# Windowed attention and two FFNs on one core: another layout of K^T, and other steps for the weight conversion

## The chip, the cores and the metric

The kernel runs on one core of a Trainium2 chip. The metric is the device time of one execution in microseconds. Three timed runs of the kernel before gave 912.32, 913.23 and 914.58 us; the median is 913.23.

## The reference

Three stages stand behind one another. Attention has 4 batches of 8 heads, 512 local and 32 global positions and a head size of 64. Local queries see the 32 global keys and the local keys at a distance of at most 32; global queries see all 544 keys.

```python
s_g = scale * q_g @ k_all^T ;  out_g = softmax(s_g) @ v_all
s_ll = where(|i - j| <= 32, scale * q_l @ k_l^T, -1e9)
s_lg = scale * q_l @ k_g^T
out_l = softmax(concat[s_lg, s_ll]) @ concat[v_g, v_l]
x = concat[out_g, out_l], as 2176 rows of 512
x = (h * cos(h)) @ w_out,  h = x @ w_in           # first FFN, 512 -> 2048 -> 512
y = relu(h)^2 @ w2_out,    h = x @ w2_in          # second FFN
```

The FFN weights come as 64-bit floats, and the kernel makes 32-bit floats of them itself ("conversion").

## The kernel before

**Attention.** A pair p is two heads of one batch; there are 16. Its work is split into items: two local items (each 256 queries of both heads) for every pair, and after two pairs one global item (the global queries of four heads). So 40 items stand in a list, ten for each batch: L L L L G L L L L G. The loop at the end of the kernel runs over steps s. In each step every kind of work is issued once, for the item or pair that lies `lag` places away, in the order of `CFG["order"]`: CV (copies of V, shifted by half a block), LQ (Q loads), S (scores on TensorE, here PE), TE (evacuation of the transposed probabilities by ScalarE, here ACT), BG (conversion: loads and part A), LK (K loads), OM (output matmuls), TRK (transposes of K), KEV (evacuation of K^T), CC (conversion part C), SM (masked scores and exps), RC (reciprocals), NM (norm), CB (conversion part B), LV (V loads), OE (output evacuation), TRQ and QE (transposes of Q and their evacuation), KC (K^T's other parts), TM (transposes of probabilities). Each engine works through its own queue in that order. Nothing overtakes on an engine: what stands behind a waiting instruction waits too.

With the lags, an item's scores are computed in step s, its norm is issued in s+1, its transposes on PE in s+2 and their evacuation on ACT in s+3, its output matmuls in s+4. K loads are issued for every second pair in steps 0, 5, 10 and so on, Q loads (four transfers) in steps 1, 6, 11, V loads (six) in steps 3, 8, 13, the copies of V in steps 1, 6, 11. In steps 5, 15 and 25 the V of the global tokens is loaded for the next batch, in 4, 14, 24 a small load for K's tail and in 7, 17, 27 the global queries (L397). All these loads and copies are issued by SP's queue, in program order.

**K^T.** `kT` holds 8 blocks of 160 columns for a pair: 64 keys of the block, 64 of the next block (a copy), 32 global keys. ACT writes the first 64 of each block out of PSUM (L336). GpSimd, here POOL, copies seven blocks into the second 64 (L351), broadcasts the global keys (L353) and copies the tail (L361). A score matmul reads the 160 columns of a block at once (L420). The local keys are laid out shifted by 32, so that a block and the next make the window of 64 queries.

**Probabilities.** VectorE (DVE) adds the mask and finds the row's extremum into `pt`, ACT takes the exponential in place with its sum (L446). The norm multiplies by the reciprocal: POOL for the global 32 columns into `pg` (L468), then the 128 window columns in place, one unit on DVE and three on POOL (L475). PE transposes them into `tw` (L488), in one of two PSUM banks that K's, Q's and the global items' transposes use too; ACT evacuates it into `tws` (L494) and `tg` into `tgs` (L498). There are four buffers of `pt`.

**Conversion.** The weights are cut into 32 groups g of two pieces each. `Feed.begin` starts at most one piece in a call and moves a pipeline of five stages: the load is issued in the step of the beginning (L126, L131), part A (POOL L143, ACT L146) two steps later, part B (DVE L154, L155) three, part C (POOL L165) four steps later. There are two buffers of the raw piece. In attention a step adds 0.5 to a credit from step 5 on, but not in steps of which the fifth next begins a new pair (`free`); a piece starts at 1.0. That gives pieces 8, 11, 14, 18, 21, 24, 28, 31, 34, 36 and 38, named here by the step of their beginning. From step 40 on FFN steps run in the same loop and add 0.5 each as well. A converted group is split into a high and a low part in two calls of `split`: two ACT copies (L228), then in a later call one subtraction on POOL and one on DVE (L214). In attention `split` is called in steps 22, 24, 27, 29 and 33; it returns where the group isn't converted.

**FFN.** 160 steps of 24 matmuls each (L757, L786), the first four of them within the attention loop. The first group of four weight groups serves five column blocks, 20 steps.

Of the kernel before, what the change touches and what calls it, by code (L numbers as in the profile page):

```python
# [10 lines left out]
F32 = mybir.dt.float32  # L11
# [3 lines left out]
AF = mybir.ActivationFunctionType  # L15
ALU = mybir.AluOpType
# [3 lines left out]
P = 128  # L20
NEG = -8.0e9
# [22 lines left out]
         'CV': 11},  # L44
 'ndv': 1,
 'teg': 'AA',
 'free': -5,
 'kb': 'P',
 'split': [22, 24, 27, 29, 33],
 'sx': [32, 34, 37, 39],  # L50
 'arate': 0.5,
 'rate': 0.5,
 's0': 5,
 'groups': [[4, 5, 7], [8, 8]],
 'xd': [0, 1, 2, 3],
 'nr': 6,
 'oe': 'DD',
 'sgb': 0}
GROUPS = CFG["groups"]
RATE, ARATE, XD, NRING = CFG["rate"], CFG["arate"], CFG["xd"], CFG["nr"]  # L60

@with_exitstack
def kernel(
# [14 lines left out]
    nc = tc.nc  # L78
# [175 lines left out]
    ep = early.enter_context(tc.tile_pool(name="ep", bufs=1))  # L254

    KTB = 2 * 64 + SG
    masks = [ep.tile([P, 160], F32, name=f"mask{i}") for i in range(3)]
    VA = [lp.tile([P, 5, 4, D], F32, name=f"va{i}") for i in range(2)]
    VB = [lp.tile([P, 4, 4, D], F32, name=f"vb{i}") for i in range(2)]
# [61 lines left out]
    def tr_k(p):  # L321
        b, kk = divmod(p, NPAIR)
        tk = bank(BT, "tk")
        for c in range(4):
            nc.tensor.transpose(  # L325
                tk[:, c * P : (c + 1) * P],
                kn[p // 2][:, c, 2 * (p % 2) : 2 * (p % 2) + 2].rearrange("p h d -> p (h d)"),
                ident,
            )
        t = ep.tile([P, 8, KTB], F32, tag="kT", name="kT", bufs=3)  # L330
        kT[p] = t
        tks[p] = tk

    def k_evac(p):
        t, tk = kT[p], tks.pop(p)
        nc.scalar.activation(  # L336
            t[:, :, 0:64], tk.rearrange("p (j q) -> p j q", q=64), AF.Copy
        )
        if CFG["kb"] == "A":
            nc.scalar.activation(  # L340
                t[:, :, 128:KTB], tk[:, 0:SG].unsqueeze(1).to_broadcast([P, 8, SG]), AF.Copy
            )
        elif CFG["kb"] == "D":
            nc.vector.tensor_copy(
                t[:, :, 128:KTB], tk[:, 0:SG].unsqueeze(1).to_broadcast([P, 8, SG])
            )

    def k_copy(p):
        t = kT[p]
        one = dict(scalar1=1.0, scalar2=1.0, op0=ALU.mult, op1=ALU.mult)  # L350
        nc.gpsimd.tensor_scalar(t[:, 0:7, 64:128], t[:, 1:8, 0:64], **one)  # L351
        if CFG["kb"] == "P":
            nc.gpsimd.tensor_scalar(  # L353
                t[:, :, 128:KTB], t[:, 0, 0:SG].unsqueeze(1).to_broadcast([P, 8, SG]), **one
            )
        if p > 1:
            k_tail(p)

    def k_tail(p):
        b, kk = divmod(p, NPAIR)  # L360
        nc.gpsimd.tensor_scalar(  # L361
            kT[p][:, 7, 64:128], ktail[:, kk, b, :], 1.0, 1.0, op0=ALU.mult, op1=ALU.mult
        )

    def tr_q(p):
# [37 lines left out]
        load_small(qgn, q_g[b], b)  # L403

    class Local:
# [4 lines left out]
        def s_mm(self):  # L413
            self.s = [bank(BS, "s") for h in range(2)]
            for i in range(2):
                for half in range(2):
                    j = 4 * self.hb + 2 * i + half
                    for h in range(2):
                        d = slice(64 * h, 64 * h + 64)
                        nc.tensor.matmul(  # L420
                            self.s[h][64 * half : 64 * half + 64, 160 * i : 160 * i + 160],
                            lhsT=qT[self.p][d, 64 * j : 64 * j + 64],
                            rhs=kT[self.p][d, j, :],
                            start=True,
                            stop=True,
                            skip_group_check=True,
                        )

        def softmax(self):
            self.pt = lp.tile([P, 4, KTB], F32, tag="pt", name="pt", bufs=4)  # L430
            self.st = lp.tile([P, 3, 4], F32, tag="st", name="st", bufs=4)

            def unit(u):
                i = 2 * self.hb + u % 2
                m = masks[1] if i == 0 else masks[2] if i == 3 else masks[0]
                nc.vector.tensor_tensor_reduce(  # L436
                    out=self.pt[:, u, :],
                    in0=self.s[u // 2][:, 160 * (u % 2) : 160 * (u % 2) + 160],
                    in1=m,
                    scale=-0.125,  # L440
                    scalar=3.0e38,
                    op0=ALU.add,
                    op1=ALU.min,
                    accum_out=self.st[:, 0, u : u + 1],
                )
                nc.scalar.activation(  # L446
                    self.pt[:, u, :],
                    self.pt[:, u, :],
                    AF.Exp,
                    bias=self.st[:, 0, u : u + 1],  # L450
                    scale=-1.0,
                    accum_out=self.st[:, 1, u : u + 1],
                )

            return [lambda u=u: unit(u) for u in range(4)]
# [10 lines left out]
        def norm(self):  # L466
            self.pg = lp.tile([P, 4, SG], F32, tag="pg", name="pg", bufs=2)
            nc.gpsimd.tensor_tensor(  # L468
                self.pg,
                self.pt[:, :, P:KTB],  # L470
                self.st[:, 2, :].unsqueeze(2).to_broadcast([P, 4, SG]),
                op=ALU.mult,
            )
            for u in range(4):
                (nc.vector if u < CFG["ndv"] else nc.gpsimd).tensor_scalar(  # L475
                    self.pt[:, u, 0:P],
                    self.pt[:, u, 0:P],
                    self.st[:, 2, u : u + 1],
                    1.0,
                    op0=ALU.mult,  # L480
                    op1=ALU.mult,
                )

        def t_mm(self):
            self.tw = bank(BT, "tw").rearrange("p (u q) -> p u q", u=4)
            self.tg = bank(BG, "tg")[:, 0:P]
            for u in range(4):
                nc.tensor.transpose(self.tw[:, u, :], self.pt[:, u, 0:P], ident)  # L488
            nc.tensor.transpose(self.tg, self.pg.rearrange("p u q -> p (u q)"), ident)

        def t_evac(self):
# [42 lines left out]
    class Global:  # L534
# [3 lines left out]
        def s_mm(self):  # L538
            self.s = []
            for n in (320, 256):  # L540
                s = bank(BT if CFG["sgb"] >> (n == 256) & 1 else BS, "sg")
                self.s.append(s)
                for i in range(2):
# [2 lines left out]
                    nc.tensor.matmul(  # L546
                        s[64 * i : 64 * i + 64, 0:n],
                        lhsT=qgbd[:, kk, self.b, :],
                        rhs=t[:, 0:5, 0:64] if n == 320 else t[:, 5:8:2, 0:128],
                        start=True,  # L550
                        stop=True,
                    )
# [96 lines left out]
    for h in range(2):  # L649
# [3 lines left out]
            compare_op=ALU.is_ge, fill=NEG, base=0, channel_multiplier=-1,  # L653
        )
        nc.gpsimd.affine_select(
            out=masks[0][s, 64:128], in_=masks[0][s, 64:128], pattern=[[-1, 64]],
            compare_op=ALU.is_ge, fill=NEG, base=0, channel_multiplier=1,
        )
    for i in (1, 2):
        nc.vector.tensor_copy(masks[i], masks[0])  # L660
    nc.vector.memset(masks[1][0:64, 0:32], NEG)
    nc.vector.memset(masks[2][64:128, 96:128], NEG)
    nc.vector.memset(qgbd, 0.0)

    nc.gpsimd.memset(ktail, 0.0)
# [238 lines left out]
    for s in range(L["TRK"], NI + L["OE"]):  # L904
        due = lambda k: due_tr.get(s - k)
        cb, qe = [], []
        for c in CFG["order"]:
            if c == "BG":
                cb = feed.begin(ARATE if due(CFG["free"]) is None else 0.0) if s >= CFG["s0"] else []
            elif c == "CB":  # L910
                for op in cb:
                    op()
# [111 lines left out]
```

## Time and profile before

| | |
|---|---|
| median of the timed runs | 913.23 us (912.32 to 914.58) |
| the profiled execution's own time | 911.74 us |
| its span | 910.0 us |
| PE busy | 890.7 us (98%) |
| weight loads of PE | 793.7 us (87%) |
| DVE, ACT, POOL busy | 502.5, 439.4, 447.8 us |
| chain that ended last, by engine | PE 91%, DVE 3%, DMA 2% |

The span is what the trace covers. A row of a timeline has the start and the length in microseconds from the span's start, the engine, the line of the kernel, the operation, what it writes and reads, the shape and how many instructions are merged; in brackets stands the idle time of its engine before it and what ended that. SPq is SP's queue, where transfers are issued; the length of such a row is the issue alone, not the transfer. A busy PE isn't PE at its peak, since matmuls are pipelined and their ends are modelled.

### The profile page before, as it was taken

The numbers are of one execution on the slowest core, as the hardware profiler recorded it, in microseconds if no ns is written. First come the engines' busy times: TensorE is split into PE (matmuls) and PEld (weight loads), VectorE is DVE, ScalarE is ACT, GpSimd is POOL, SyncE is SP. The second block draws the span as 40 slices with busy tenths as digits, with TensorE's granted clock in tenths as the row PEclk, the third lists the DMA queues.
The fourth block names the chain that finished last, engine by engine and source line by source line (L and its number), as shares of the span: only waits on it lengthen the run. The fifth ranks groups of instructions, "written<-read, shape, count | busy, mean of one in ns | idle before, by whom it ended". The sixth has DMA issues, their size and how long they took to land.

```text
span 910.0 us, 15436 instructions
## 1 busy us (share of the span) xinstructions
PE 890.7 (98%) x5720; PEld 793.7 (87%) x5720; DVE 502.5 (55%) x1058; ACT 439.4 (48%) x1036; POOL 447.8 (49%) x517
## 2 busy tenths in 40 slices
PE   7899999999999999999999999999999999999997
PEld 5777777999999999999999988889999888899996
DVE  5687899866776666765554483433422833232221
ACT  5778787665655545545444553333334632222211
POOL 4577888754574435744342484444423842222221
PEclk9999999999999999999999999999999999999999
DMA  7888643221122111121110021111100101010001
GB/s 168 192 192 195 165 129 94 71 70 53 49 62 70 47 53 61 50 70 47 47 47 1 1 70 47 53 44 66 47 1 1 47 1 47 1 47 1 35 35 36
DMA packets 82075, 57.10 MB, mean 63 GB/s; under 512 B 58320, under 2 KB 74704, under 8 KB 82000
## 3 DMA queue, kind: packets, MB, share of 16 engines
q1 hardware_dynamic: 79824, 55.59, 22.0%
q8 instruction: 45, 0.74, 0.3%
q10 hardware_dynamic: 2176, 0.52, 0.3%
q14 instruction: 30, 0.25, 0.1%
HBM read 47.45 MB, written 4.46 MB: 57 GB/s over the span
## 4 chain that ended last, share of the span: by engine, by line
PE 91%; DVE 3%; DMA 2%; ACT 1%; SPq 1%; POOL 1%; issue 1%; ACTq 0%; POOLq 0%; DVEq 0%
PE h L757 41%; PE y L786 41%; PE s L420 2%; PE tw L488 1%; PE o L504 1%; PE tq L368 1%; DVE pt L436 1%; PE o L516 1%; PE og L622 1%; DMA raw<-in_moe_w_out_dram 1%; PE sg L546 1%; PE tk L325 0%; ACT pt L446 0%; SPq L292 0%; PE twg L603 0%
## 5 line engine op out<-in xcount | busy, mean ns | idle before, releaser
L757 PE MATMUL h<-x,w 128*128 128x436 f32 (+3 forms) x1920 | 403.4, 358 | 0.0
L857 POOL TENSOR_TENSOR glo<-cr,ghi 128x436 fp32r<-128x436 f32 (+3 forms) x160 | 186.8, 1167 | 407.7 <-ACT ghi L851 393.9
L757 PEld LDWEIGHTS h<-x,w 128*128 128x128 f32 x1920 | 354.6, 188 | 27.5
L786 PE MATMUL y<-ghi,w 128*128 128x436 f32 (+1 forms) x640 | 177.6, 358 | 0.0
L846 DVE TENSOR_TENSOR cr<-h,cr 128x436 f32<-128x436 f32 (+3 forms) x160 | 96.6, 605 | 134.0 <-ACT cr L837 115.0
L786 PE MATMUL y<-w,ghi 128*128 128x512 f32 x544 | 168.4, 390 | 0.0
L745 DVE TENSOR_TENSOR x<-xt,x 128x436 fp32r<-128x436 f32 (+3 forms) x100 | 102.5, 1035 | 93.3 <-ACT x L744 78.3
L837 ACT ACTIVATE cr<-h 128x384 f32<-128x384 f32 (+1 forms) x80 | 42.8, 535 | 210.7 <-PE h L757 209.4
L786 PEld LDWEIGHTS y<-ghi,w 128*128 128x128 f32 x640 | 120.3, 188 | 6.1
L786 PEld LDWEIGHTS y<-w,ghi 128*128 128x128 f32 x544 | 101.4, 188 | 18.9
L786 PE MATMUL y<-glo,w 128*128 128x436 f32 (+1 forms) x320 | 114.8, 359 | 0.0
L786 PE MATMUL y<-w,glo 128*128 128x512 f32 x272 | 106.8, 393 | 0.0
L851 ACT ACTIVATE ghi<-cr 128x436 fp32r<-128x436 f32 (+3 forms) x160 | 89.7, 560 | 24.5 <-DVE cr L846 23.6
L831 ACT ACTIVATE ck<-h 128x436 int32<-128x436 f32 (+1 forms) x80 | 42.6, 532 | 113.1 <-PE h L757 113.1
L833 DVE SCALAR_TENSOR_TENSOR cr<-h,ck 128x436 f32<-128x436 f32 (+1 forms) x80 | 48.6, 607 | 84.9 <-ACT ck L831 84.9
L165 POOL TENSOR_TENSOR r<-cu,cc 128x512 uint32<-128x512 uint32 x64 | 85.0, 1328 | 2.0 <-DVE cc L155 2.0
L744 ACT ACTIVATE x<-xt 128x436 fp32r<-128x436 f32 (+3 forms) x100 | 55.1, 560 | 20.2 <-PE h L757 19.9
L786 PEld LDWEIGHTS y<-glo,w 128*128 128x128 f32 x320 | 60.1, 188 | 2.7
L786 PEld LDWEIGHTS y<-w,glo 128*128 128x128 f32 x272 | 51.0, 188 | 10.8
L842 ACT ACTIVATE cr<-cr,halfpi 128x436 f32<-128x436 f32 (+1 forms) x80 | 52.5, 657 | 10.1 <-DVE cr L833 10.1
L155 DVE SCALAR_TENSOR_TENSOR cc<-raw,cc 128x512 uint32<-128x512 uint32 x64 | 55.7, 870 | 0.0
L446 ACT ACTIVATE pt<-pt,st 128x160 f32<-128x160 f32 x128 | 53.3, 425 | 4.1 <-DVE st L436 4.1
(91 smaller groups left out, 907.4 us busy)
## 6 DMA issues: line engine op xcount, KB each, us to landing
raw<-in_moe_w_in_dram SPq DMA_DIRECT2D x32, 512.0 KB, 3.7
raw<-in_moe_w_out_dram SPq DMA_DIRECT2D x32, 512.0 KB, 3.5
vb<-va SPq DMA_DIRECT2D x16, 256.0 KB, 4.6
out_dram<-ypart SPq DMA_DIRECT2D x16, 256.0 KB, 2.1
qn<-in_q_l_dram SPq DMA_DIRECT2D x28, 128.0 KB, 3.7
va<-in_v_l_dram SPq DMA_DIRECT2D x24, 128.0 KB, 3.3
kn<-in_k_l_dram SPq DMA_DIRECT2D x21, 128.0 KB, 3.0
va<-in_v_l_dram SPq DMA_DIRECT2D x8, 96.0 KB, 3.2
```

Source lines behind the costliest of these rows:

```text
L155: lambda: v.scalar_tensor_tensor(c, t[:, :, 1].bitcast(U32), 0x80000000, c, op0=ALU.bitwise_and, op1=ALU.bitwise_or,),
L165: nc.gpsimd.tensor_tensor(ring[g][:, q, :].bitcast(U32), u, c, op=ALU.add)
L446: nc.scalar.activation(self.pt[:, u, :], self.pt[:, u, :], AF.Exp, bias=self.st[:, 0, u : u + 1], scale=-1.0, accum_out=self.st[:, 1, u : ...
L744: nc.scalar.activation(hi, xr, AF.Copy)
L745: return lambda: (nc.vector if kk in XD else nc.gpsimd).tensor_tensor(lo, xr, hi.bitcast(F32), op=ALU.subtract)
L757: nc.tensor.matmul(h, lhsT=w[:, ws, 0, kk * P : (kk + 1) * P], rhs=x, start=(k == 0), stop=(k == 3 * NK - 1),)
L786: nc.tensor.matmul(o, lhsT=l, rhs=r, start=(c_first and k == 0), stop=(c_last and k == 2))
L833: lambda: nc.vector.scalar_tensor_tensor(r, h, INV2PI, k, op0=ALU.mult, op1=ALU.subtract),
L842: nc.scalar.activation(ctmp[s], ctmp[s], AF.Sin, bias=halfpi, scale=TWOPI)
L846: nc.vector.tensor_tensor(r, hps.pop(s), r, op=ALU.mult)
L851: nc.scalar.activation(ghi[s], ctmp[s], AF.Copy)
L857: nc.gpsimd.tensor_tensor(lo, ctmp.pop(s), hi.bitcast(F32), op=ALU.subtract)
```

## The change

K^T becomes one row of nine places of 96 columns: 64 keys of a block and 32 global keys behind them. A score matmul reads 160 columns from the start of a place: the block, the global keys, and the next block. So blocks are no longer copied; the ninth place holds the tail. The masks and `pt` follow that order (64, 32, 64), `pt` gets a fifth unit of space and three buffers instead of four. The norm of the window columns writes to a new tile `pn` (two buffers), which the transposes read.

The conversion's beginnings in attention are now a list of steps, and the calls of `split` move. From step 40 on the attention loop begins no piece any more, only the FFN steps do.

```diff
- 'free': -5,
- 'split': [22, 24, 27, 29, 33],
+ 'split': [15, 21, 25, 31, 35],
- 'arate': 0.5,
+ 'begin': [6, 9, 14, 16, 19, 24, 26, 29, 34, 36],
- 's0': 5,
...
+    GK = slice(64, 64 + SG)
...
-        t = ep.tile([P, 8, KTB], F32, tag="kT", name="kT", bufs=3)
+        t = ep.tile([P, 9, 64 + SG], F32, tag="kT", name="kT", bufs=3)
...
     def k_evac(p):
         nc.scalar.activation(
-            t[:, :, 0:64], tk.rearrange("p (j q) -> p j q", q=64), AF.Copy
+            t[:, 0:8, 0:64], tk.rearrange("p (j q) -> p j q", q=64), AF.Copy
         )
...
     def k_copy(p):
-        nc.gpsimd.tensor_scalar(t[:, 0:7, 64:128], t[:, 1:8, 0:64], **one)
-        if CFG["kb"] == "P":
-            nc.gpsimd.tensor_scalar(
-                t[:, :, 128:KTB], t[:, 0, 0:SG].unsqueeze(1).to_broadcast([P, 8, SG]), **one
-            )
+        nc.gpsimd.tensor_scalar(
+            t[:, 0:8, GK], t[:, 0, 0:SG].unsqueeze(1).to_broadcast([P, 8, SG]), **one
+        )
...
     def k_tail(p):
-            kT[p][:, 7, 64:128], ktail[:, kk, b, :], 1.0, 1.0, op0=ALU.mult, op1=ALU.mult
+            kT[p][:, 8, 0:64], ktail[:, kk, b, :], 1.0, 1.0, op0=ALU.mult, op1=ALU.mult
...
+    def windows(t, u):
+        return t.rearrange("p u q -> p (u q)")[:, KTB * u : KTB * u + 192].rearrange(
+            "p (a q) -> p a q", a=2
+        )[:, :, 0:64]
...
     class Local, s_mm:
-                            rhs=kT[self.p][d, j, :],
+                            rhs=kT[self.p].rearrange("p j q -> p (j q)")[d, 96 * j : 96 * j + KTB],
...
-            self.pt = lp.tile([P, 4, KTB], F32, tag="pt", name="pt", bufs=4)
+            self.pt = lp.tile([P, 5, KTB], F32, tag="pt", name="pt", bufs=3)
...
     norm:
-                self.pt[:, :, P:KTB],
+                self.pt[:, 0:4, GK],
...
+            self.pn = lp.tile([P, 4, P], F32, tag="pn", name="pn", bufs=2)
             for u in range(4):
                 (nc.vector if u < CFG["ndv"] else nc.gpsimd).tensor_scalar(
-                    self.pt[:, u, 0:P],
-                    self.pt[:, u, 0:P],
+                    self.pn[:, u].rearrange("p (a q) -> p a q", a=2),
+                    windows(self.pt, u),
...
     t_mm:
-                nc.tensor.transpose(self.tw[:, u, :], self.pt[:, u, 0:P], ident)
+                nc.tensor.transpose(self.tw[:, u, :], self.pn[:, u], ident)
...
     class Global, s_mm:
-                        rhs=t[:, 0:5, 0:64] if n == 320 else t[:, 5:8:2, 0:128],
+                        rhs=t[:, 0:5, 0:64] if n == 320 else t[:, 5:9, 0:64],
...
     the loop over steps:
-                cb = feed.begin(ARATE if due(CFG["free"]) is None else 0.0) if s >= CFG["s0"] else []
+                cb = feed.begin(1.0 if s in CFG["begin"] else 0.0)
```

The masks' second half moves from columns 64:128 to 96:160, and the branches of `k_evac` for another value of `kb`, which were not taken, are gone.

## Rows read from the trace of the kernel before

**Rows 1.** Grouped lines of PE, 162 us to the end: busy, mean ns | idle before.

```profile
L757 PE MATMUL h<-x,w 128*128 128x436 f32 (+3 forms) x1872 | 393.0, 358 | 0.0
```

**Rows 2.** Timeline of PE: score matmuls that open steps 13, 14, 16, 17, 19, 21, 23, 27, 33, 37.

```profile
51.30 0.77 PE L420 MATMUL s<-kT,qT 64*64 64x160 f32 x16
55.14 1.19 PE L546 MATMUL sg<-kT,qgbd 128*64 128x320 f32 x8
...
62.83 0.78 PE L420 MATMUL s<-kT,qT 64*64 64x160 f32 x16
65.64 0.77 PE L420 MATMUL s<-kT,qT 64*64 64x160 f32 x16
...
72.01 1.19 PE L546 MATMUL sg<-kT,qgbd 128*64 128x320 f32 x8
...
78.77 0.77 PE L420 MATMUL s<-kT,qT 64*64 64x160 f32 x16
...
84.11 0.77 PE L420 MATMUL s<-kT,qT 64*64 64x160 f32 x16
...
100.34 0.77 PE L420 MATMUL s<-kT,qT 64*64 64x160 f32 x16
...
119.04 0.77 PE L420 MATMUL s<-kT,qT 64*64 64x160 f32 x16
...
134.21 0.77 PE L420 MATMUL s<-kT,qT 64*64 64x160 f32 x16
```

**Rows 3.** Timeline of ACT: in steps 8, 13, 18 and 28.

```profile
38.06 0.43 ACT L446 ACTIVATE pt<-pt,st 128x160 f32<-128x160 f32 x1
...
55.92 0.69 ACT L146 ACTIVATE cc<-raw 128x512 uint32<-128x512 uint32 x1 [2.17 <-DMA raw<-in_moe_w_out_dram]
...
70.88 0.43 ACT L446 ACTIVATE pt<-pt,st 128x160 f32<-128x160 f32 x1
...
105.57 0.42 ACT L446 ACTIVATE pt<-pt,st 128x160 f32<-128x160 f32 x1
```

**Rows 4.** Timeline of PE: transposes in steps 9, 14, 19, 23 and 41.

```profile
41.72 0.60 PE L488 MATMUL tw<-ident,pt 128*128 128x128 f32 x4
...
58.80 0.66 PE L488 MATMUL tw<-ident,pt 128*128 128x128 f32 x4 [0.98 <-ACT tws L494]
...
74.53 0.60 PE L488 MATMUL tw<-ident,pt 128*128 128x128 f32 x4
...
87.49 0.98 PE L368 MATMUL tq<-ident,qn 128*128 128x128 f32 x4 [0.61 <-ACT tws L494]
...
151.00 0.28 PE L606 MATMUL tlg<-ident,ptg 128*32 128x128 f32 x1 [0.68 <-ACT tgs L498]
```

**Rows 5.** SP's queue: three issues, and a row of its waits (total, times, longest).

```profile
37.38 0.51 SPq L397 DMA_DIRECT2D qgn<-in_q_g_dram  x1
...
69.08 0.50 SPq L397 DMA_DIRECT2D qgn<-in_q_g_dram  x1
...
101.92 0.51 SPq L397 DMA_DIRECT2D qgn<-in_q_g_dram  x1
...
SPq L299 <- PE og L622: 16.6, 4, 8.7
```

**Rows 6.** DMA issues at 28 to 42 and 86 to 103 us: size, microseconds to landing.

```profile
raw<-in_moe_w_in_dram SPq DMA_DIRECT2D x1, 512.0 KB, 5.1
...
raw<-in_moe_w_in_dram SPq DMA_DIRECT2D x1, 512.0 KB, 3.9
```

**Rows 7.** Two stretches: length, busy time of PE, PEld, DVE, ACT, POOL, granted clock, DMA.

```profile
58.80:64.00 5.20, 5.20 (x76) 4.04 (x78) 4.41 (x20) 3.93 (x16) 5.14 (x9) 1.00 1.08 224
87.50:91.00 3.50, 3.50 (x15) 2.41 (x17) 1.75 (x5) 2.95 (x12) 2.15 (x6) 0.53 0.80 169
```

**Rows 8.** Grouped lines of POOL by form, 0 to 160 us: busy, mean ns | idle before.

```profile
L468 POOL TENSOR_TENSOR pg<-pt,st 128x128 f32<-128x128 f32 x32 | 13.0, 405 | 31.8 <-DVE st L463 26.0 <-DVE pt L475 3.5 <-ACT tws L494 1.2
...
L351 POOL TENSOR_SCALAR kT<-kT 128x448 f32<-128x448 f32 x16 | 9.4, 588 | 4.5 <-ACT kT L336 4.5
```

More of the change, by code (lines that the diff above doesn't have):

```diff
@@ L59 @@
 GROUPS = CFG["groups"]
-RATE, ARATE, XD, NRING = CFG["rate"], CFG["arate"], CFG["xd"], CFG["nr"]
+RATE, XD, NRING = CFG["rate"], CFG["xd"], CFG["nr"]
 @with_exitstack
@@ L336, in k_evac @@
         nc.scalar.activation(
-            t[:, :, 0:64], tk.rearrange("p (j q) -> p j q", q=64), AF.Copy
+            t[:, 0:8, 0:64], tk.rearrange("p (j q) -> p j q", q=64), AF.Copy
         )
-        if CFG["kb"] == "A":
-            nc.scalar.activation(
-                t[:, :, 128:KTB], tk[:, 0:SG].unsqueeze(1).to_broadcast([P, 8, SG]), AF.Copy
-            )
[L343 to L346, printed above, removed]
     def k_copy(p):
@@ L350, in k_copy @@
         one = dict(scalar1=1.0, scalar2=1.0, op0=ALU.mult, op1=ALU.mult)
-        nc.gpsimd.tensor_scalar(t[:, 0:7, 64:128], t[:, 1:8, 0:64], **one)
-        if CFG["kb"] == "P":
-            nc.gpsimd.tensor_scalar(
-                t[:, :, 128:KTB], t[:, 0, 0:SG].unsqueeze(1).to_broadcast([P, 8, SG]), **one
-            )
+        nc.gpsimd.tensor_scalar(
+            t[:, 0:8, GK], t[:, 0, 0:SG].unsqueeze(1).to_broadcast([P, 8, SG]), **one
+        )
         if p > 1:
@@ L655 @@
         nc.gpsimd.affine_select(
-            out=masks[0][s, 64:128], in_=masks[0][s, 64:128], pattern=[[-1, 64]],
+            out=masks[0][s, 96:160], in_=masks[0][s, 96:160], pattern=[[-1, 64]],
             compare_op=ALU.is_ge, fill=NEG, base=0, channel_multiplier=1,
@@ L661 @@
     nc.vector.memset(masks[1][0:64, 0:32], NEG)
-    nc.vector.memset(masks[2][64:128, 96:128], NEG)
+    nc.vector.memset(masks[2][64:128, 128:160], NEG)
     nc.vector.memset(qgbd, 0.0)
```

## The prediction

> **What bounds the kernel now.** I read the profile in three moves. First TensorE (PE) in the FFN, in the grouped lines from 162 us on: its groups have no idle time in front of them; the costliest stands for all [rows 1]. Nothing that the other engines do there sets the end, so the change can only move the moment at which the FFN starts. Second, the starts of the score matmuls on PE, which mark the 40 attention steps (step s holds the scores of item s) [rows 2]. PE repeats its work every ten steps, so equal steps of different decades can be compared: steps 14 and 15 took 62.83 - 55.14 = 7.69 us, their twins 19 and 20 took 78.77 - 72.01 = 6.76. Steps 13 to 16 took 65.64 - 51.30 = 14.34; without those 0.93 us, 13.41. Steps 23 to 26 took 100.34 - 84.11 = 16.23 and 33 to 36 took 134.21 - 119.04 = 15.17. So PE has a floor, and what lies above it is waiting. Third, the timelines of ScalarE (ACT) and PE at the excess of steps 14 and 15: ACT sat 2.17 us until the weights of conversion piece 11 (begun in step 11) had landed, then had its conversion, four exps and an evacuation to do [rows 3], and PE got its next transposes at 58.80 after 0.98 us of nothing [rows 4]. A piece's part A, two steps after its beginning, stands in ACT's queue ahead of the four exps of that step. A late landing therefore blocks the softmax, and behind it the evacuation of `tw`, on which PE's next transposes wait for a bank.
>
> **The change, part by part.**
>
> Where the pieces begin. Q loads are issued at lag 1, for every second pair: in steps 1, 6, 11, 16, and so on, ahead of the piece of that step (order CV, LQ, S, TE, BG). So of the new beginnings 4, 6 and 9 of each ten, 4 and 9 are free of K, Q and V, but 6 is not: pieces 6, 16 and 26 come right behind four Q transfers, in 16 and 26 behind the copies of V too, and shortly behind K and the V of the global tokens. In SP's queue that is the place where the global queries (L397) stand: 37.38, 69.08 and 101.92 us [rows 5]. The old pieces 8, 18 and 28 are issued just behind these, so little is gained in issue time, while part A moves two whole steps earlier.
>
> Piece 6 (a). The old piece 8 took 5.1 us to land from that place [rows 6]: 37.38 + 5.1 = 42.5. ACT comes to part A of step 8 at 38.06, where the exps now start [rows 3], so it stands 4.4 us, and VectorE, GpSimd (POOL) and the exps behind it stand too. From the start of a late part A to the transposes (conversion, four exps, evacuation) piece 11 took 58.80 - 55.92 = 2.88 [rows 3, 4]: 42.48 + 2.88 = 45.36. Those transposes (item 7) now start at 41.72 [rows 4]: 3.6 us lost. With the fastest landing shown, 3.9 us [rows 6], it is 2.4; a landing 0.3 later gives 3.9. I take 3.6.
>
> Piece 16 (b). 69.08 + 5.1 = 74.2 against ACT's 70.88 [rows 3]: transposes of item 17 at 77.06 where they start at 74.53 [rows 4], 2.5 lost as the old run lies. In the new run V's loads move with PE, since they wait for the global output matmuls `og` [rows 5], while piece 11 no longer delays PE by 0.93 between: up to 3.5. Against it, the transfers that piece 11 used to hold up are out of the way, for which no row gives a size: down to 0. I take 2.0, near the row.
>
> Piece 26 (c). 101.92 + 3.9 = 105.8 against 105.57 [rows 3, 5, 6]: almost in time, but the old PE came there late by the 2.8 us of steps 23 to 26 (16.23 - 13.41). If PE gains these, the wait is up to 2.5; if not, 0. I take 1.4.
>
> The clock (d). The granted TensorE clock was 0.53 of full speed, mostly the 1.2 GHz level, from 87.5 to 91 [rows 7], right behind 0.61 us of idle PE at 87.49 [rows 4]. That costs half of some 3.4 us, 1.7. Piece 6 leaves PE idle six times as long; I count one fall, 1.7 (0 to 5.1 for three), since PE's idle 0.98 us at 58.80 [rows 4] brought none [rows 7]. The Trainium skill, TensorE: Matmul & The Clock Gate, section "HAM oscillation — how this bites in real kernels", speaks against the change more strongly: in a loop where PE waits for a transfer each time, the clock gate falls back to half rate in every such wait, and the work behind it starts cold. By that rule the three new waits would bring three falls, 5.1 instead of 1.7.
>
> The splits (e). g0 moves from step 22 to 15, g1 from 24 to 21, g2 from 29 to 31; the second halves fall in 21, 25 and 35. Each is two ACT copies, now in or next to a step with a part A. ACT has slack for one such neighbour; 0.4 (0 to 1).
>
> What goes away. Piece 11's wait: 0.93 (f). Steps 23 to 26 lose the splits of 22 and 24 and the clock fall: at most 2.8; a split in 21 and piece 24 stay, so 2.3, and at least 0.5 (g). Steps 33 to 36: at most 15.17 - 13.41 = 1.8; the half split of step 33 moves to 35 and piece 31 goes, the slices of x stay: 1.1, at least 0 (h). The crossing to the FFN: three pieces fewer (12 instead of 15 begun by step 43), but pieces 34 and 36, beside which the last norms run, are in both lists. The wait of 0.68 for ACT [rows 4] is the bound, 0.3 the value (i).
>
> The POOL copies. Sixteen copies of 0.59 us go, 9.4 us in all, and nothing is added: the broadcast of 256 and the tail of 64 elements stay. But POOL stands 31.8 us ahead of its first norm operation, 26.0 of it for VectorE's reciprocal [rows 8]. The time is freed where POOL waits anyway: 0, at best 1.0 inside the crowded steps of (g) and (h).
>
> Costs of nothing. Score matmuls keep 160 contiguous columns and the masks their size; both norms read two runs of 64 in place of one of 128, 0 (the POOL broadcast already runs over eight pieces). `pt` with three buffers is last read by the norm, one step after it is written, not by the transposes two steps after: the same slack. The new `pn` has two buffers, so a norm waits for the transposes of two items before. Behind it would stand POOL's K broadcast and part C of a piece; but ahead of that norm VectorE runs the softmax of the step, whose scores PE computes after those transposes, so they are done by then. If that cover went, a norm would wait for one step's transposes, under 1 us. In the FFN the pieces run three behind; the first weights of the second group are needed 20 FFN steps after its start, so 0 there.
>
> **The sum.** Lost 3.6 + 2.0 + 1.4 + 1.7 + 0.4 = 9.1; gained 0.9 + 2.3 + 1.1 + 0.3 = 4.6; net +4.5 on the profiled execution's 911.74 us: 916.2. That execution lies 1.5 below the median 913.23, so the forecast is 917.7, 0.5% slower. A measurement tells about 0.3%, 2.7 us, from no change.
>
> **The rivals.**
> - *Faster: the crowded steps pay more than the landings cost.* Place: steps 23 to 26 and 33 to 36, with POOL's freed time worth its 1.0. It decides if pieces 16 and 26 land before ACT is free and the clock does not fall. Lost 3.6 + 0.4, gained 0.9 + 2.8 + 1.8 + 0.7 + 1.0 = 7.2: -3.2, 910.0. For it: SP had waits before its V loads, so an emptier queue could deliver earlier. Against: 3.3 us are missing at step 18.
> - *No change.* (b) and (c) at half, no clock fall: 3.6 + 1.0 + 0.7 + 0.4 = 5.7 against 4.6: 914.3.
> - *The clock falls at each of the three waits.* 3.4 more than the forecast: 921.1. For it: 0.61 us of idle PE were followed by a fall. Against: 0.98 at 58.80 were not. The page on the clock gate in the Trainium skill, named at (d), has this case as its rule; the trace agrees for the one wait and not for the other.
> - *The change does what its words say.* If pieces 6, 16 and 26 landed as freely as the others, (a) to (d) would go: 0.4 - 4.6 = -4.2, 909.0. The order of SP's queue speaks against it.
>
> **How the numbers follow.** Forecast 0.42, clock at each wait 0.16, no change 0.22, crowded steps 0.15, words 0.05. Slower by over 0.3% (above 916.0): 0.42 + 0.16 = 0.58; within: 0.22; faster: 0.20. Leaving out about the outer half of the first and of the last two cases, the range is 909.5 to 921.5; the likeliest case's own is 915 to 920.
>
> **What would show it.** Right: ACT standing some 4 us for `raw` near 38 us, PE near 41.7 idle for over 3 us behind ACT's `tws`, and shorter stands in steps 18 and 28; a granted clock under 1 behind the first; step 14 at its floor. Wrong: `raw` landed before ACT's part A in step 8, or PE passing these transposes without idling; steps 23 to 26 as long as before; FFN with idle PE.

## The result: 1.4% slower, and the profile after

The changed kernel took 925.65 us (median of four, 925.21 to 927.18) against 912.78 for the kernel before in the same measurement: ratio 1.0142, 95% interval 1.0122 to 1.0162. The forecast of 917.7 has the sign right and a third of the size, and 925.65 lies outside its range of 909.5 to 921.5. The profiled execution took 925.21 us, its span is 923.4, so it stands 13.4 above the span before.

Where the 13.4 lie shows in the starts of PE's steps, the same steps as in [rows 2]: timeline of PE after, the score matmuls that open steps 13, 16, 17, 21, 23, 26, 27, 33 and 37, and the first FFN matmuls.

```profile
55.55 0.77 PE L415 MATMUL s<-kT,qT 64*64 64x160 f32 x16
66.14 0.77 PE L415 MATMUL s<-kT,qT 64*64 64x160 f32 x16
69.53 0.77 PE L415 MATMUL s<-kT,qT 64*64 64x160 f32 x16
87.83 0.78 PE L415 MATMUL s<-kT,qT 64*64 64x160 f32 x16
93.17 0.78 PE L415 MATMUL s<-kT,qT 64*64 64x160 f32 x16
104.02 0.78 PE L415 MATMUL s<-kT,qT 64*64 64x160 f32 x16
106.83 0.77 PE L415 MATMUL s<-kT,qT 64*64 64x160 f32 x16
129.93 0.77 PE L415 MATMUL s<-kT,qT 64*64 64x160 f32 x16
145.97 0.78 PE L415 MATMUL s<-kT,qT 64*64 64x160 f32 x16
158.14 2.62 PE L753 MATMUL h<-x,w 128*128 128x436 f32 x12
```

The kernel before, four more rows of its PE timeline: the key tails' transposes in step 6, the score matmuls that open steps 25 and 26, and the first FFN matmuls.

```profile
30.75 0.41 PE L380 MATMUL ttail<-ident,ktn 32*128 32x32 f32 x4 [1.75 <-DMA ktn<-in_k_l_dram]
93.41 0.48 PE L420 MATMUL s<-kT,qT 64*64 64x160 f32 x2
97.01 0.77 PE L420 MATMUL s<-kT,qT 64*64 64x160 f32 x16
146.06 2.62 PE L757 MATMUL h<-x,w 128*128 128x436 f32 x12
```

Stretch by stretch, from these rows and [rows 2]:

| stretch | before | after | difference | forecast |
|---|---|---|---|---|
| start to step 13 | 51.30 | 55.55 | +4.25 | +5.3 (a, d) |
| 13 to 17 | 14.34 | 13.98 | -0.36 | -0.9 (f) |
| 17 to 21 | 13.13 | 18.30 | +5.17 | +2.0 (b) |
| 21 to 27 | 21.57 | 19.00 | -2.57 | -2.3 (g) |
| 27 to 33 | 18.70 | 23.10 | +4.40 | +1.4 (c) |
| 33 to 37 | 15.17 | 16.04 | +0.87 | -1.1 (h) |
| 37 to the FFN | 11.85 | 12.17 | +0.32 | -0.3 (i), and 0.4 (e) somewhere |
| FFN, to the end of the span | 763.94 | 765.26 | +1.32 | 0 |

Three stretches carry the loss, and each has one of the three pieces in it. In the first, the piece is only half of it: PE is 2.26 us late already at the start of step 9 (41.46 against 39.20), before it waits for piece 6. So it is a coincidence that this stretch comes near its forecast. Timeline of ACT after, the answer to [rows 3]: part A of pieces 6, 16 and 26, with ACT's idle time in brackets.

```profile
43.30 0.69 ACT L144 ACTIVATE cc<-raw 128x512 uint32<-128x512 uint32 x1 [2.88 <-DMA raw<-in_moe_w_in_dram]
79.61 0.66 ACT L144 ACTIVATE cc<-raw 128x512 uint32<-128x512 uint32 x1 [4.75 <-DMA raw<-in_moe_w_out_dram]
116.18 0.66 ACT L144 ACTIVATE cc<-raw 128x512 uint32<-128x512 uint32 x1 [4.01 <-DMA raw<-in_moe_w_in_dram]
```

And PE after, the answer to [rows 4]: its idle times from step 6 to step 36 of 0.6 us and more.

```profile
31.48 0.41 PE L369 MATMUL ttail<-ident,ktn 32*128 32x32 f32 x4 [3.51 <-DMA ktn<-in_k_l_dram]
46.17 0.66 PE L484 MATMUL tw<-ident,pn 128*128 128x128 f32 x4 [2.04 <-ACT tws L490]
82.45 0.94 PE L484 MATMUL tw<-ident,pn 128*128 128x128 f32 x4 [3.87 <-ACT tws L490]
119.02 0.87 PE L484 MATMUL tw<-ident,pn 128*128 128x128 f32 x4 [3.15 <-ACT tws L490]
134.59 1.08 PE L484 MATMUL tw<-ident,pn 128*128 128x128 f32 x4 [1.20 <-DVE qgbd L383]
```

Rows two to four are the mechanism that was forecast: load late, ACT late, `tw` bank late, PE idle. Rows one and five were not foreseen. With four of these waits the clock went to its lower level. Windows of the profile after (columns as in [rows 7]):

```profile
31.96:35.37 3.41, 3.41 (x37) 2.86 (x39) 0.42 (x1) 3.06 (x13) 0.00 (x0) 0.50 0.83 217
46.00:50.00 4.00, 3.83 (x53) 3.10 (x54) 3.68 (x14) 3.79 (x16) 3.77 (x7) 1.00 1.16 265
83.16:86.57 3.41, 3.41 (x42) 2.65 (x41) 2.96 (x12) 2.64 (x12) 3.41 (x7) 0.50 1.12 230
120.70:124.11 3.41, 3.41 (x36) 3.02 (x31) 2.33 (x15) 2.26 (x10) 3.41 (x8) 0.50 0.23 77
134.36:137.77 3.41, 3.18 (x13) 1.94 (x15) 2.92 (x15) 2.40 (x10) 1.46 (x4) 0.50 0.85 209
```

A granted clock of 0.50 is the 1.2 GHz level. It stands behind the waits of 3.51, 3.87 and 3.15 us, begins 0.2 us before the end of the one of 1.20, and doesn't stand behind the one of 2.04. The kernel before had one such stretch in its attention.

### The profile page after: what moved, and what is told of

Read it like the earlier page. It is cut to its first block, busy times and chain, and to the rows that moved or that the text cites. A ratio compares the mean times of both kernels' runs of the same rounds, so it can differ in the third digit from the quotient of the medians.

```text
span 923.4 us, 15402 instructions
## 1 busy us (share of the span) xinstructions
PE 896.7 (97%) x5720; PEld 797.2 (86%) x5720; DVE 504.1 (55%) x1058; ACT 440.0 (48%) x1036; POOL 440.9 (48%) x501
## 3 DMA queue, kind: packets, MB, share of 16 engines
HBM read 47.45 MB, written 4.46 MB: 56 GB/s over the span
## 4 chain that ended last, share of the span: by engine, by line
PE 89%; DMA 3%; DVE 3%; SPq 2%; ACT 2%; POOL 1%; issue 1%; POOLq 0%; DVEq 0%
PE h L753 41%; PE y L782 41%; PE s L415 2%; PE o L500 1%; DMA raw<-in_moe_w_in_dram 1%; PE o L512 1%; PE tw L484 1%; DVE pt L431 1%; ACT pt L441 1%; DMA raw<-in_moe_w_out_dram 1%; DMA qn<-in_q_l_dram 1%; POOL pn L471 1%; SPq L301 1%; SPq L291 0%; PE og L618 0%
## 5 line engine op out<-in xcount | busy, mean ns | idle before, releaser
L741 DVE TENSOR_TENSOR x<-xt,x 128x436 fp32r<-128x436 f32 (+3 forms) x100 | 110.4, 1115 | 97.0 <-ACT x L740 82.0
L141 POOL TENSOR_SCALAR cu<-raw 128x512 f32<-128x512 f32 x64 | 50.7, 792 | 13.4 <-DMA raw<-in_moe_w_in_dram 7.9
```

Of the source, the lines that this page charges most:

```text
L141: nc.gpsimd.tensor_scalar(u, t[:, :, 1].bitcast(F32), 2.0**-112, 1.0, op0=ALU.mult, op1=ALU.mult)
L741: return lambda: (nc.vector if kk in XD else nc.gpsimd).tensor_tensor(lo, xr, hi.bitcast(F32), op=ALU.subtract)
```

## The experiments

Ratios are to the kernel before, run in turn on the same chip, with 95% intervals.

**Which half of the change costs.** Two kernels, each with one half.

```diff
 # layout_only: the changed kernel, with the old rule for beginnings and the old splits
- 'begin': [6, 9, 14, 16, 19, 24, 26, 29, 34, 36],
+ 'free': -5, 'arate': 0.5, 's0': 5,
- 'split': [15, 21, 25, 31, 35],
+ 'split': [22, 24, 27, 29, 33],
...
- cb = feed.begin(1.0 if s in CFG["begin"] else 0.0)
+ cb = feed.begin(ARATE if due(CFG["free"]) is None else 0.0) if s >= CFG["s0"] else []
```

> The new layout of K^T, `pt` and `pn` with the old conversion: credits, pieces 8, 11, 14, 18, 21, 24, 28, 31, 34, 36, 38 and splits in 22, 24, 27, 29, 33. Landing theory (the loss is made by pieces 6, 16 and 26, whose weights land after ACT has reached their part A, and by the falls of PE's clock behind these waits): no loss, 911 to 914 us, ACT's one wait for raw weights of some 2 us in step 13 as before. Layout theory (the norm out of place, fewer buffers, or the strided K^T cost time in every step): at least 5 us over the kernel before, 918 to 926, with longer local steps.

Measured: 915.00, ratio 1.0026 (1.0004 to 1.0049).

```diff
 # schedule_only: the kernel before, with the new beginnings and splits
- cb = feed.begin(ARATE if due(CFG["free"]) is None else 0.0) if s >= CFG["s0"] else []
+ cb = feed.begin(1.0 if s in CFG["begin"] else 0.0)
...
- 'split': [22, 24, 27, 29, 33],
+ 'split': [15, 21, 25, 31, 35],
+ 'begin': [6, 9, 14, 16, 19, 24, 26, 29, 34, 36],
```

> The old layout with the new list of beginnings and the new splits. Landing theory: the whole loss, 923 to 928 us; ACT waits 3 to 5 us for raw weights in steps 8, 18 and 28, and three or four clock falls. Layout theory: within 4 us of the kernel before, 911 to 917.

Measured: 923.45, ratio 1.0133 (1.0095 to 1.0171). Its PE idles at the same three places, though its keys lie as before (timeline of PE):

```profile
47.88 1.11 PE L488 MATMUL tw<-ident,pt 128*128 128x128 f32 x4 [3.48 <-ACT tws L494]
85.43 1.11 PE L488 MATMUL tw<-ident,pt 128*128 128x128 f32 x4 [3.36 <-ACT tws L494]
122.83 1.13 PE L488 MATMUL tw<-ident,pt 128*128 128x128 f32 x4 [3.02 <-ACT tws L494]
```

With each of the three the granted clock was 0.50 for 6.5 us or more. The schedule makes nearly all of the loss; the layout by its interval 0.04% to 0.49%. The schedule has the new splits in it too; they stay in begin8, begin7 and load_first below, where most of the loss goes, so they are not what made it.

**Later beginnings.**

```diff
 # begin8: the three pieces two steps later; begin7: one step later (7, 17, 27)
- 'begin': [6, 9, 14, 16, 19, 24, 26, 29, 34, 36],
+ 'begin': [8, 9, 14, 18, 19, 24, 28, 29, 34, 36],
```

> The changed kernel with pieces 6, 16 and 26 begun in steps 8, 18 and 28 instead, all else as changed. Their issue stays at nearly the same place of SP's queue, behind the Q loads; only their part A moves two steps later. Landing theory: the three waits go and with them their clock falls; 910 to 915 us. A rival, that the transfers themselves are the load (ten pieces early, beside the K, Q and V transfers, whatever the step of part A): still 920 to 926 us.

> The changed kernel with the pieces of steps 6, 16 and 26 begun in steps 7, 17 and 27, the first steps after the Q loads; all else as changed. Theory 1 (what counts is how many transfers are still in the queue when the load is issued and two steps of 6 to 7 us for it to land): one step later brings most of it back, waits under 1 us, 914 to 918. Theory 2 (the three pieces cost because they and the pieces of steps 9, 19 and 29 are closer together than before): two steps apart instead of three, so as slow as the changed kernel or slower, 924 or more.

Measured: begin8 915.82 (1.0034, 1.0013 to 1.0055), begin7 915.94 (1.0047, 1.0027 to 1.0068). In begin8 PE no longer waits for ACT behind these pieces. In begin7 three remain behind ACT, 1.19, 2.02 and 1.41 us, now in front of score matmuls; half the sum of the changed kernel's. So two steps are too few for a load from that place in the queue, three nearly enough. Closer pieces as such (7 and 9, or 8 and 9, instead of 6 and 9) did not bring the loss back; all three variants of the changed kernel, with load_first below, still stay 0.3% to 0.5% above the kernel before, and what that rest is was not found.

**One piece alone.** The kernel before with piece 18 begun in step 16.

```diff
- def begin(self, rate):
+ def begin(self, rate, extra=0.0):
...
-     self.credit = min(self.credit + rate, 1.5)
+     self.credit = min(self.credit + rate, 1.5) + extra
...
+ rate = ARATE if due(CFG["free"]) is None else 0.0
+ cb = feed.begin(rate, {16: 1.0, 18: -1.0}.get(s, 0.0)) if s >= CFG["s0"] else []
```

> The kernel before with one edit: the conversion piece that begins in step 18 begins in step 16 instead, behind the Q loads of that step; all other pieces, the key layout and the splits stay as before (its two later parts move two steps earlier with it). Theory 1 (a load put behind the step's other transfers lands more than two steps later, the scalar engine waits for it in front of its evacuations, and the wait is paid in full): landing 5 to 6 us after its issue, a wait of 3 to 4 us on TensorE in step 18 or 19, the offset against the kernel before grows by 3.5 to 4.5 us there, and the end comes 3 to 5 us later (916 to 918). Theory 2 (the price in the changed kernel comes from three such pieces and the two-step backlog together; alone one is worth what the prediction gave it): about 2.0 us, 914 to 915.5. If only the average occupancy of the queue counts: no change.

Measured: 918.60, ratio 1.0062 (1.0040 to 1.0083). The wait was paid in full, as theory 1 said; what the prediction gave it was too little. PE at the starts of steps 19 and 21 of this kernel and at its wait, and the window behind the wait:

```profile
73.11 1.19 PE L546 MATMUL sg<-kT,qgbd 128*64 128x320 f32 x8
79.59 1.04 PE L488 MATMUL tw<-ident,pt 128*128 128x128 f32 x4 [3.80 <-ACT tws L494]
84.91 0.77 PE L420 MATMUL s<-kT,qT 64*64 64x160 f32 x16
```

```profile
80.10:83.51 3.41, 3.39 (x39) 2.55 (x40) 2.89 (x14) 2.58 (x12) 3.41 (x9) 0.50 0.84 204
```

Steps 19 and 20 took 84.91 - 73.11 = 11.80 us against 78.77 - 72.01 = 6.76 [rows 2]: 5.04 more, of which 3.80 is the wait; 1.24 is more work time, most of it at half clock. PE was 1.10 us late at step 19 already: this execution too had the key tails' wait and a clock fall in step 6, ahead of anything that the edit touches.

**What the clock costs.** PE kept at work in the wait: first in the changed kernel, then in the one with piece 18 moved.

```diff
 # keep_busy: the changed kernel; in steps 9, 19 and 29, ahead of the transposes
...
+ for k in range(14):
+     nc.tensor.matmul(obank[:, 384:512], lhsT=ident, rhs=ident, ...)
 # one_moved_busy: one_moved; in step 19, ahead of the transposes, in a free score bank
+ fill = bank(BS, "fill")[:, 0:P]
+ for k in range(14):
+     nc.tensor.matmul(fill, lhsT=ident, rhs=ident, ...)
```

> The changed kernel with 14 extra matmuls of 128x128 (some 2.9 us by their cost of about 0.2 each) in steps 9, 19 and 29, ahead of the transposes that wait for ACT, written to an unused part of an output bank: PE is kept at work while it would wait. The landings stay late. If the clock falls behind the waits cost time of their own, the falls at 83 and 121 us go and the time falls by 2 to 3.4 us, to 922 to 924 (the extra matmuls overshoot the 2.0 us wait of step 9 by up to 0.9). If the falls are hidden by other engines: 925 to 927, with the clock at 1.00 after steps 19 and 29.

Measured: 939.98, ratio 1.0311 (1.0278 to 1.0345). The filling work waited itself, 4.86, 4.69 and 5.04 us, for VectorE's reading of the bank, and the transposes came only behind it. It says nothing of the clock.

> The kernel with piece 18 moved to step 16 (918.6; TensorE waits 3.80 us at 79.59 for the evacuation, and the clock is at half for 3.41 us from 80.10), with 14 matmuls of 128x128 of no use put ahead of the waiting transposes of step 19, in a score bank that is free by then; they add work and leave the wait's cause. Theory 1 (the clock falls because TensorE stood idle, and that is a second price on top of the wait): no fall at 80, steps 19 and 20 together 10.6 us instead of 11.8, and 1.2 us less at the end. Theory 2 (the falls come and go for other reasons, and the wait alone is the price): the fall stays, or goes without a gain. If the filling work itself has to wait, as it did in another bank, steps 19 and 20 grow by up to 3 us, and the run says nothing of the clock.

Measured: 917.31, ratio 1.0057 (1.0036 to 1.0078). Here the work ran inside the wait. PE at the same places, and the window:

```profile
73.74 1.19 PE L546 MATMUL sg<-kT,qgbd 128*64 128x320 f32 x8
76.25 3.29 PE L959 MATMUL fill<-ident 128*128 128x128 f32 x28
80.01 0.90 PE L488 MATMUL tw<-ident,pt 128*128 128x128 f32 x4 [0.47 <-ACT tws L494]
84.47 0.77 PE L420 MATMUL s<-kT,qT 64*64 64x160 f32 x16
```

```profile
79.00:83.00 4.00, 3.38 (x42) 2.27 (x43) 3.13 (x11) 3.37 (x13) 4.00 (x10) 1.00 0.97 205
```

ACT still stood 4.45 us for the load, but the clock stayed at 1.00 and steps 19 and 20 took 10.73 us, 1.07 less, with useless work added. Of these, 0.86 lie behind the wait (84.91 - 79.59 = 5.32 against 84.47 - 80.01 = 4.46), the rest ahead of it, where the load came 0.2 us sooner. So with the idle time filled this fall did not come, and it had cost about 0.9 us.

A second price stands in step 23, where nothing is filled: PE waits 0.61 us there in the kernel before [rows 4], 0.59 in the moved one and in the one just shown, and the clock fell in the first two only (in the moved one 0.50 from 93.75 to 97.16). Step 23, the wait, step 25 and the window of the kernel with filled idle time:

```profile
89.81 0.77 PE L420 MATMUL s<-kT,qT 64*64 64x160 f32 x16
93.18 0.66 PE L368 MATMUL tq<-ident,qn 128*128 128x128 f32 x4 [0.59 <-ACT tws L494]
97.47 0.48 PE L420 MATMUL s<-kT,qT 64*64 64x160 f32 x2
```

```profile
92.00:97.00 5.00, 4.41 (x64) 3.63 (x62) 3.78 (x19) 4.15 (x15) 2.27 (x6) 1.00 0.64 127
```

Steps 23 and 24 took 97.47 - 89.81 = 7.66 us without a fall, 93.41 - 84.11 = 9.30 in the kernel before and 9.28 in the moved one: here a fall cost 1.6 us. And the same short wait came with a fall or without one, so at waits of that length something else decides. These prices rest on the traces; the ratios of the two kernels, 1.0062 and 1.0057, have overlapping intervals.

**The place in the queue.** The changed kernel, with the three loads ahead of V copies and Q loads.

```diff
+ if job not in raw:
      conv_load(*job)
...
+ if s in (6, 16, 26):
+     conv_load(*feed.jobs[0])
  for c in CFG["order"]:
```

> The changed kernel with one edit: in steps 6, 16 and 26 the conversion's load is issued ahead of the step's V copies and Q loads instead of behind them; its later parts stay where they are. Theory 1 (the place in the issuing queue decides when the piece lands, and nothing else about these steps costs): the load is issued 4 to 6 us earlier, lands before the scalar engine asks for it, the three waits of 2.0, 3.9 and 3.2 us and most of the clock falls that go with them vanish; 925.65 goes to 913 to 917. Theory 2 (what costs is the sum of transfers in these steps: the Q blocks or the V copies are late in the place of the piece): a new wait on Q, V or K of 2 us or more in steps 7 to 9, 17 to 19 and 27 to 29, and the time stays above 920.

Measured: 914.83, ratio 1.0050 (1.0027 to 1.0073), range 912.74 to 921.40. The steps, the parts and their number are those of the changed kernel; only the issue moved, and 10.8 of 12.9 us went by the medians, 8.4 by the ratios. The two differ because eight of its twelve runs took 912.7 to 915.4 us and four 919.4 to 921.4; the trace is of one of the eight, so what the four have is open. Of the three waits 0.68 us is left in its profile, behind piece 6; new are 0.83 and 1.10 us in the steps behind pieces 9 and 19. Its FFN begins at 146.07, where that of the kernel before does (146.06); the 1.4 us by which its profile is longer lie in the FFN.

**The key tails.** The kernel before with their small loads two steps earlier, and then both kernels with that and with all conversion loads first.

```diff
- if s in (4, 14, 24):
+ if s in (2, 12, 22):
      load_ktn(s // 10 + 1)
...
 # first_ktn, first_ktn_new: also, ahead of a step's other work, if it begins a piece
+     conv_load(*feed.jobs[0])
```

> The kernel before with one edit: the loads of the key tails (64 KB each) are issued in steps 2, 12 and 22 instead of 4, 14 and 24, ahead of the V loads instead of behind them. In the changed kernel's trace TensorE waits 3.51 us for the first of them (1.75 us in the kernel before), though the change doesn't touch it. Theory 1 (the end of this wait is set by the transfer, so that time won ahead of it is given back, and it costs what it lasts): the wait goes, 1.5 to 2.5 us less, 910.5 to 911.5, and a clock fall at that place becomes rarer. Theory 2 (something else is due at the same moment: the K blocks behind it, or the scores' operands): no change within 0.5 us.

Measured: 915.36, ratio 1.0031 (1.0012 to 1.0049): slower, which neither theory had. The wait of step 6 went, PE came to step 14 at 53.36 instead of 55.14, and there (timelines of ACT and PE):

```profile
57.60 0.66 ACT L146 ACTIVATE cc<-raw 128x512 uint32<-128x512 uint32 x1 [5.63 <-DMA raw<-in_moe_w_out_dram]
60.44 1.11 PE L488 MATMUL tw<-ident,pt 128*128 128x128 f32 x4 [4.40 <-ACT tws L494]
```

Piece 11, 0.98 us of idle PE in the kernel before [rows 4], cost 4.40: PE came 1.8 us earlier and the load landed 1.7 later (57.6 instead of 55.9; issued 0.95 later, at 51.44, and 0.7 longer under way); the granted clock was 0.50 for 6.8 us from 58.57. Of the 3.1 us by which its profile is longer, 1.4 lie in the FFN.

> The kernel before (old key layout, old beginnings) with two edits: every conversion load of the attention is issued ahead of its step's other transfers, and the key tails are loaded two steps earlier. With the key tails alone earlier, the 1.8 us won in step 6 came back as a longer wait for piece 11, which landed at 57.6 instead of 55.9 (TensorE waited 4.40 instead of 0.98 us). Theory 1 (a load's place in the issuing queue is what sets its landing): with the piece ahead of V copies and Q loads, neither wait is left; 2.5 to 3 us less than before in the attention, 908 to 910. Theory 2 (the transfers together bound these steps, whatever their order): the time won in step 6 is given back at the next V, Q or K block, 911 to 915.

Measured: 911.78, ratio 0.9986 (0.9971 to 1.0002). No wait above 0.6 us is left between steps 6 and 33 in its profile, and its FFN begins at 144.39, 1.67 us earlier than before; it also lacks the clock fall of step 23, which is worth as much. The direction is theory 1's, the gain too small to tell from none.

> The changed kernel (new key layout, its ten beginnings and splits) with the same two edits: all ten conversion loads issued first in their steps, the key tails two steps earlier. With the loads of steps 6, 16 and 26 alone first it ran at 914.8, its FFN beginning where that of the kernel before does. Theory 1: the key-tail wait goes too (2 to 3.5 us where it occurs), and the new schedule's own gains in steps 23 to 26 show: 909 to 912. Theory 2 (bounded by the transfers together): 913 to 916, with a new wait on a Q, V or K block in the steps behind.

Measured: 918.75, ratio 1.0063 (1.0041 to 1.0085): both theories were too low. Without the key tails' wait, PE reached step 9 at 37.45; load 6 was still issued only at 38.08, behind K and V, and PE stood again (timelines of ACT and PE):

```profile
42.18 0.66 ACT L144 ACTIVATE cc<-raw 128x512 uint32<-128x512 uint32 x1 [5.77 <-DMA raw<-in_moe_w_in_dram]
45.02 1.12 PE L485 MATMUL tw<-ident,pn 128*128 128x128 f32 x4 [4.89 <-ACT tws L491]
```

In load_first PE reached step 6 at 30.99, here at 28.24. So load_first owed part of its success at piece 6 to PE being late there: with PE on time, the first place in step 6 was too late too.

**The FFN's pace.**

```diff
 # shifted: the kernel before, its V tiles 3456 bytes lower
+ pad = lp.tile([P, 864], F32, name="pad")
```

> The kernel before with one edit: an unused tile of 3456 bytes per partition in the attention's pool, so that the V tiles lie 3456 bytes lower, as they do with the new layout. In the kernel before the first FFN block runs at 4.64 us for 24 matmuls of 436 columns, in all three profiles with the new layout at 4.75 us, though every FFN tile has the same address in both. Theory 1 (the place of the attention's tiles sets it): 4.75 us in the first block, the FFN 1.3 to 1.5 us longer. Theory 2 (it is not the place, but the order or the phase in which TensorE's work arrives with the new layout): 4.64 us as in the kernel before, no difference.

Measured: one run, 911.01. Windows of the first FFN block, of the kernel before and of this one, and this one's first FFN matmuls:

```profile
180.00:210.00 30.00, 30.00 (x157) 29.12 (x156) 20.85 (x33) 18.11 (x36) 16.28 (x15) 1.00 0.22 70
```

```profile
180.00:210.00 30.00, 30.00 (x154) 28.49 (x153) 18.74 (x31) 17.84 (x36) 15.77 (x14) 1.00 0.18 55
```

```profile
146.50 2.62 PE L758 MATMUL h<-x,w 128*128 128x436 f32 x12
```

154 matmuls in 30 us where the kernel before has 157, as theory 1 wanted; but from the first FFN matmul to the end of the span it is 909.2 - 146.50 = 762.7 us, 1.2 less than before, where theory 1 wanted 1.3 to 1.5 more. And one_moved, with the old layout and nothing shifted, has 153 in such a window, so the place isn't the cause. Over all profiles this FFN took 762.7 us (shifted, first_ktn), 763.9 (the kernel before, schedule_only) or 765.2 to 765.3 (the others): all three lengths occur with the old layout. What sets them stays open.

## Why the prediction was wrong

The mechanism was the right one: piece loads behind Q transfers land too late for a part A two steps on, ACT blocks, PE stands. The three experiments that take this away by another step (begin8, begin7) or another place in the queue (load_first) bring back 9.7 to 10.8 of the 12.9 us by the medians, 8.4 to 9.9 by the ratios. The size failed in steps (b), (c) and (d), and small things were missed: of the 8.9 us by which the profiles' 13.4 exceed the sum's 4.5, the stretches of (b) and (c) hold 3.2 and 3.0, a clock fall in each, that of (h) 2.0 and the FFN 1.3.

- **(b) and (c), the steps that failed.** I took 2.0 and 1.4 near old rows; PE stood 3.87 and 3.15. Two things were wrong. First, the issue did not stay where [rows 5] had it relative to PE: load 16 was issued 73.53 - 66.14 = 7.4 us after step 16 began (the old place: 69.08 - 62.83 = 6.2), load 26 6.7 us after step 26 (4.9). Second, landing took 6.1 and 5.4 us, not the 5.1 and 3.9 of [rows 6]; the nine piece loads that the kernel before issued between 37 and 125 us took 3.9 to 5.9. SP's rows of the profile after, the one of its V loads in step 23 among them, the two landings, and the same V loads of the kernel before:

```profile
73.53 0.38 SPq L129 DMA_DIRECT2D raw<-in_moe_w_out_dram  x1
95.41 0.33 SPq L298 DMA_DIRECT2D va<-in_v_g_dram  x1
110.76 0.38 SPq L124 DMA_DIRECT2D raw<-in_moe_w_in_dram  x1
```

```profile
raw<-in_moe_w_out_dram SPq DMA_DIRECT2D x1, 512.0 KB, 6.1
```

```profile
raw<-in_moe_w_in_dram SPq DMA_DIRECT2D x1, 512.0 KB, 5.4
```

```profile
86.34 0.33 SPq L299 DMA_DIRECT2D va<-in_v_g_dram  x1
```

  The wait at (c) divides so: at the old places the load would have been 0.7 us late for ACT (step 26 at 104.02, plus 4.9, plus 3.9, against ACT free at 112.17); 1.8 of later issue and 1.5 of slower landing make 4.0, and ACT stood 4.01. The later issue comes from the V loads. They go out 2.2 us behind the start of step 23 in both kernels (95.41 - 93.17, 86.34 - 84.11), since they wait for the global output matmuls, and the piece's place follows 15.4 and 15.6 us behind them (110.76, 101.92). So load 26 hangs on the start of step 23, and what PE gains in steps 23 to 25, (97.01 - 84.11) - (104.02 - 93.17) = 2.05 us, doesn't move it: PE waits for it at piece 26. Steps 13 to 15 and piece 16 are alike (V loads at 53.53 and 57.78, 2.2 us behind step 13 in both; 0.94 gained). The sum counted these gains in full, as (f) and (g), and yet took (b) and (c) below the 3.5 and 2.5 that the prediction gave for just that case. With 3.5 and 2.5 it would have been 2.6 higher, 920.3. The argument for taking less in (b), that the transfers piece 11 had held up would be out of the way, shows in no row here. The bound of 3.5 for (b) was nearly right as a value; the bound of 2.5 for (c) was too low, since it kept the landing at 3.9.
- **(a)** forecast 3.6, PE idle 2.04. Piece 6 landed nearly as forecast, 43.3 (issued at 37.61, 5.7 to land) against 42.5, but PE came 2.26 us later to it, behind the key tails' wait and a clock fall in step 6.
- **The key tails** were not in the sum. PE reached step 6 at 27.19, 1.04 earlier than before, and waited for a load until 31.48 (before: 30.75), which was issued 0.75 later (28.12, 27.37) and took no longer to land. Step 6 took 7.7 us instead of 4.6, and the clock fell behind the wait. Most of this is not the change's: one_moved is the kernel before up to step 16, and it waited there too, had a granted clock of 0.50 from 32.5 to 35.5, and reached step 7 at 34.20, where the kernel before is at 32.84 and the changed one at 34.88:

```profile
31.29 0.41 PE L380 MATMUL ttail<-ident,ktn 32*128 32x32 f32 x4 [1.69 <-DMA ktn<-in_k_l_dram]
34.20 1.35 PE L420 MATMUL s<-kT,qT 64*64 64x160 f32 x16
```

  That a gain ahead of a landing is given back is shown by the early key tails, where it came back at piece 11.
- **(d)** one fall forecast; four came, one before. Of the four, the one in step 6 came in old-layout kernels too, and the one in step 33 lies at no piece's load. At 0.9 to 1.6 us each, three more are 2.6 to 4.9 us. The price of 1.7 was near the dearer of the two measured; the count was too low. The rival with a fall at every wait came nearest, 921.1, and was still short, because (b) and (c) were. The Trainium skill, TensorE: Matmul & The Clock Gate, section "HAM oscillation — how this bites in real kernels", says that a loop which waits some 3 to 5 us for a transfer again and again falls to half clock at each wait; the trace agrees for the two pieces with waits of such a length, 3.87 and 3.15 us (0.50 at 83.16 and 120.70), and piece 6, with a shorter wait of 2.04, had no fall (1.00 from 46 to 50).
- **(f), (g)** right in kind: piece 11's wait went (no idle PE in step 14), and steps 21 to 26 gained 2.57 against 2.3. Of the first, 0.58 came back in step 16. Of the second, 1.6 are the clock fall of step 23, and that was the luck of one profile: layout_only, shifted, ktn_early and first_ktn have the old pieces and no fall there, and took 19.9 to 20.3 us for these steps, the changed kernel 19.00. So the change itself gained 0.9 to 1.3 there.
- **(h)** wrong in sign: steps 33 to 36 lost 0.87 instead of gaining 1.1. Part C of piece 29 on POOL (132.20, 1.27 us) stands beside VectorE's slice of x (132.23, 1.71 us), and the global queries' copy on VectorE (133.86) is late behind it. PE stood 1.20 us for that copy, with a clock fall. begin8 has the same wait in steps 23 and 33 (0.91 and 1.07 us). That the neighbour on POOL causes it was not tried by itself. **(e)**, the splits, was not tried by itself either.
- **The POOL copies** at nothing: no gain shows, layout_only is 0.04% to 0.49% slower, and 1.4 of the 2.0 us by which its profile is longer lie in the FFN. **The FFN** at nothing: 1.3 us of the profiles' difference lie there, but its length changes as much between kernels with the old layout, so it says little about this change. **No change, crowded steps, words true** all fell with the three waits.

## What to carry to other kernels

Price a moved load by where it stands in its queue and by when its consumer asks, and let both the issue and the landing slip as far as the rows allow: when the engine that the queue waits for is delayed, the queue is delayed with it. Time won ahead of a wait that a landing ends is not won; look for the next landing before counting it. If a sum counts a gain, it has to count the wait that the gain runs into as well. A wait of TensorE in this attention cost its length and, where the clock fell with it, 0.9 to 1.6 us on top.

## What the runs showed of the hardware that was not expected

The clock fell with an idle time of 1.20 us (134.59) and did not fall with one of 2.04 (46.17), in the same profile, and fell or did not fall with one of 0.6 us in step 23: the length of a short wait alone doesn't decide it. All fourteen waits of TensorE of 2.35 us or more between 25 and 165 us in the profiles here came with a fall. The same matmuls of 128x436 ran, at a granted clock of 1.00 and with no idle time, 157 or 154 in 30 us, in kernels whose FFN is the same, and the whole FFN took 762.7, 763.9 or 765.3 us. A load of 512 KB took 3.3 to 6.1 us to land in the attention of the two kernels; issued ahead of its step's other loads (first_ktn, 40 to 128 us) it took 3.9 to 6.4, so the place in the step alone doesn't set it.
